# Running MLP block 1 between the two halves of block 0 in a fused attention and MLP kernel

## The chip, the cores and the metric

The kernel runs on one core of a Trainium2 chip. The metric is the device time of one execution in microseconds, the median of several runs. TensorE (PE in the profile) does the matrix products, VectorE (DVE), ScalarE (ACT) and GpSimd (POOL) the elementwise work, and SyncE (SP) issues the transfers.

## The reference

Kernelized attention for 8 batches of 8 heads, 576 positions and 64 channels, then a two-layer MLP over the 4608 tokens that it leaves.

```
def phi(x):                       # x: [b, h, s, 64], w_phi: [64, 128]
    proj = x @ w_phi
    proj = proj - max(abs(proj), over the 128 features)
    return concat(exp(proj), exp(-proj))
kv  = phi(k)^T v ; z = sum over s of phi(k)
out = (phi(q) kv) / (phi(q) z + 1e-6)          # per head
x   = out as [4608 tokens, 512]                # 8 heads x 64 channels
h   = x @ w_in                                 # 512 -> 2048
y   = max(0.01 * h, h) @ w_out                 # 2048 -> 512
```

All inputs and outputs are fp32.

## The kernel before, in words

**MLP.** The 4608 tokens are cut into 18 blocks of 256, the 2048 hidden features into 16 groups of 128. A *step* is one pair (block i, group ft), 288 in all. Step n calls `layer1(i, ft)`: 12 matmuls into one PSUM tile `h` of 128 features by 256 tokens (hi times hi, hi times lo and lo times hi of an fp32 number that is split into two fp32r numbers, for four 128-row parts of the 512 channels). ScalarE then applies the leaky ReLU (L606) and casts to `gh`, VectorE subtracts to get `gl` (L608). `LAG` = 3 steps later `layer2` multiplies `gh` and `gl` by the group's rows of `w_out`: 6 matmuls of 512 columns into two PSUM tiles `acc`, which hold the sums of a block's two token halves over its 16 groups. After the last group `acc` is copied to `o` (one half on ScalarE, one on VectorE) and written out. There are two `h` tiles and two `acc` tiles, so a block's second-layer sums can start only when the copies of the block before have been made.

**Split.** Before a block's first step `split(i)` reads its 256 tokens from `ring`, the SBUF tile that holds the attention result of two batches, and writes `xh` (four casts on ScalarE) and `xl` (four subtractions on GpSimd). There is one `xh` and one `xl`. A batch has 576 tokens: blocks 0 and 1 lie wholly in batch 0, block 2 takes its last 64 and the first 192 of batch 1.

**Weights.** `load_weights()` loads `w_in` and `w_out` group by group, 32 tiles of 512 KB, through two staging buffers: two of the four head-pair rows of batch 1 in `ring`, and `qh`. Each tile is rounded and split into hi and lo by two ScalarE reads (L159, L164), four VectorE operations (L160, L161, L162, L165), a ScalarE cast (`w0h`, `w1h`) and a VectorE subtraction (`w0l`, `w1l`).

**Attention.** Heads go in pairs, four pairs to a batch. `k_phase(i)` makes the key-value sums of pair i (its transposed result is kept in one tile `kvh`), `token_q_phase(i)` (pairs 4 to 7) or `q_phase(i)` the queries: three units of 256, 256 and 64 tokens for pairs 4 to 7, each closed on GpSimd by the multiplication `ring<-ring,mb` with the reciprocal of the denominator. Pairs 0 to 3 are done ahead of the MLP. `advance(goal)` emits attention work between the steps, at a pace set by the step's number n.

**Order.** The order in which instructions stand on each engine is made by the Tile scheduler from the order of emission, from priorities (attention before weights before MLP) and from its own timeline. On the chip each engine takes its instructions in that order and waits at each for its inputs.

Of the kernel before, what the change touches and what calls it, by code (L numbers as in the profile page):

```python
# [9 lines left out]
F32 = mybir.dt.float32  # L10
# [4 lines left out]
ALU = mybir.AluOpType  # L15
AX = mybir.AxisListType

P = 128
B, H, S, D = 8, 8, 576, 64
NP = H // 2  # L20
F = 128
U = 288
DM = 512
DFF = 2048
NFT = DFF // P
T = 256
TT = T // P
NTOK = B * S
NBLK = NTOK // T
LAG = 3  # L30
NN = 8
NK = 8
NF = 12
# [12 lines left out]
def attention_moe_kernel(ctx: ExitStack, tc: tile.TileContext, q, k, v, vt, w_phi, w_in, w_out, out):  # L46
    nc = tc.nc
# [4 lines left out]
    def ct(shape, dt, name):  # L52
        return cp.tile(shape, dt, tag=name, name=name)

    def st(shape, dt, tag):
        return sp.tile(shape, dt, tag=tag, name=tag, bufs=BUFS.get(tag, 1))
# [3 lines left out]
    def pick(key):  # L60
        n = cnt[key] = cnt.get(key, -1) + 1
        e = ENG.get(key, "")
        return e[n % len(e)] if e else None

    def copy_(key, o, i):
        e = pick(key) or "a"
        if e == "a":
            nc.scalar.copy(o, i)  # L68
        else:
            (nc.vector if e == "v" else nc.gpsimd).tensor_copy(o, i)  # L70

    def tt_(key, o, a, b, op):
        (nc.vector if pick(key) == "v" else nc.gpsimd).tensor_tensor(o, a, b, op=op)  # L73

    def pt(tag):
        return ps.tile([P, 512], F32, tag=tag, name=tag, bufs=PBUFS[tag])
# [5 lines left out]
    def weight(which, part, ft):  # L82
        g, f = divmod(ft, 4)
        if (which, part, g) not in weights:
            name = f"w{which}{part}{g}"
            weights[which, part, g] = (cp.tile([P, 4, DM], F32R, tag="late", name=name, bufs=4) if g == 3 else
                                       ct([P, 4, DM], F32R, name))
        return weights[which, part, g][:, f]
# [53 lines left out]
    for j in range(2):  # L142
        r = slice(64 * j, 64 * j + 64)
# [46 lines left out]
    def k_phase(i):  # L190
        nat, plain = i < NK, i < NF
        rk, rv = kraw.pop(i)
        if not plain:
            ks = st([P, 2, S], F32R, "ks")
            for j in range(2):
                o, n = slice(64 * j, 64 * j + 64), slice(64 - 64 * j, 128 - 64 * j)
# [16 lines left out]
        for g in range(3):  # L213
            w = 2 if g < 2 else 1
            r = slice(0, P) if g < 2 else slice(64, P)
            n = P if g < 2 else 64
# [8 lines left out]
            else:  # L225
                for s in range(w):
                    t0 = (2 * g + s) * P if g < 2 else S - P
                    pk = pt("a")
                    for j in range(2):
                        nc.tensor.matmul(pk[:, 256 * j : 256 * j + 256], lhsT=ks[:, j, t0 : t0 + P],  # L230
                                         rhs=wq.rearrange("p a f -> p (a f)"), start=True, stop=True)
# [13 lines left out]
            for s in range(w):  # L245
                c = 2 * g + s
                ek = st([P, 2, 256], F32, ("ek", "kph", "kpl")[c % 3] if nat else "ek")
# [30 lines left out]
        for j in range(2):  # L278
            for t in range(2):
                nc.tensor.transpose(kvtv[:, j, t], kvs[:, j, t], ident[0:66, 0:66])  # L280
        if i < NN:
            kvh = st([P, 2, 2, P], F32, "kvh")
            nc.scalar.copy(kvh[:, :, :, 0:64], kvtv[:, :, :, 0:64])
            nc.scalar.copy(kvh[:, :, :, 64:P], kvtv[:, :, :, 64:65].broadcast_to([P, 2, 2, 64]))
            kvs_of[i] = kvh, None
        else:
            kvh = st([P, 2, 2, P], F32R, "kvh")
            kvl = st([P, 2, 2, P], F32R, "kvl")
            zb = kvtv[:, :, :, 64:65].broadcast_to([P, 2, 2, 64])
            copy_("kvh", kvh[:, :, :, 0:64], kvtv[:, :, :, 0:64])  # L290
            copy_("kvh", kvh[:, :, :, 64:P], zb)
            nc.vector.tensor_tensor(kvl[:, :, :, 0:64], kvtv[:, :, :, 0:64], kvh[:, :, :, 0:64].bitcast(F32), op=ALU.subtract)
            nc.vector.tensor_tensor(kvl[:, :, :, 64:P], zb, kvh[:, :, :, 64:P].bitcast(F32), op=ALU.subtract)
            kvs_of[i] = kvh, kvl
# [274 lines left out]
    def attention():  # L569
        for i in range(NP, B * NP + 1):  # L570
            gens = [k_phase(i)] if i < B * NP else []
            if i > NP:
                gens.append((token_q_phase if i - 1 < NN else q_phase)(i - 1))
            while gens:
                for it in list(gens):
                    if next(it, end) is end:
                        gens.remove(it)
                    else:
                        yield i - 1
            yield i  # L580

    accs = {}
    gs = {}

    def split(i):
        for d in range(NP):
            t0 = 0
            while t0 < T:
                c = (i * T + t0) % (2 * S)
                n = min(T - t0, S - c % S)  # L590
                x = ring[:, c // S, d, c % S : c % S + n]
                t1 = t0 + n
                copy_("xh", xh[:, d, t0:t1], x)
                tt_("xl", xl[:, d, t0:t1], x, xh[:, d, t0:t1].bitcast(F32), ALU.subtract)
                t0 = t1

    def layer1(i, ft):
        ph = pt("h")[:, 0:T]
        for d in range(NP):
            nc.tensor.matmul(ph, lhsT=weight(0, "h", ft)[:, d * P : d * P + P], rhs=xh[:, d], start=d == 0, stop=False)  # L600
            nc.tensor.matmul(ph, lhsT=weight(0, "l", ft)[:, d * P : d * P + P], rhs=xh[:, d], start=False, stop=False)  # L601
        for d in range(NP):
            nc.tensor.matmul(ph, lhsT=weight(0, "h", ft)[:, d * P : d * P + P], rhs=xl[:, d], start=False, stop=d == NP - 1)  # L603
        gh = st([P, T], F32R, "gh")
        gl = st([P, T], F32R, "gl")
        nc.scalar.activation(ph, ph, AF.Prelu, alpha=0.01)  # L606
        copy_("gh", gh, ph)
        nc.vector.tensor_tensor(gl, ph, gh.bitcast(F32), op=ALU.subtract)  # L608
        gs[i, ft] = (gh, gl)

    def layer2(i, ft, half=range(TT)):
        if (i, 0) not in accs:
            for t in range(TT):
                accs[i, t] = pt("acc")
        gh, gl = gs[i, ft]
        for t in half:
            ts = slice(t * P, t * P + P)
            a = accs[i, t]
            nc.tensor.matmul(a, lhsT=gh[:, ts], rhs=weight(1, "h", ft), start=ft == 0, stop=False)  # L619
            nc.tensor.matmul(a, lhsT=gh[:, ts], rhs=weight(1, "l", ft), start=False, stop=False)  # L620
            nc.tensor.matmul(a, lhsT=gl[:, ts], rhs=weight(1, "h", ft), start=False, stop=ft == NFT - 1)  # L621
        if ft == NFT - 1:
            for t in half:
                o = st([P, DM], F32, "ek" if i == NBLK - 1 and t else "o")
                copy_("o", o, accs[i, t])
                r = i * T + t * P
                nc.sync.dma_start(out[r : r + P, :], o)

    stream = attention()
    state = {"p": PA, "n": NP - 1}  # L630
# [1 line left out]
    def advance(goal):  # L632
        keep = tc.cur_priority
        tc.cur_priority = state["p"]
        while state["n"] < goal:
            state["n"] = max(state["n"], next(stream, B * NP))
        state["p"] = tc.cur_priority
        tc.cur_priority = keep

    def room(i):  # L640
        return min(B, 2 + i * T // S) * NP
# [12 lines left out]
    tc.cur_priority = PW  # L654
    load_weights()
    tc.cur_priority = 0
    steps = [(i, ft) for i in range(NBLK) for ft in range(NFT)]
    split(0)
    for n, (i, ft) in enumerate(steps):
        layer1(i, ft)  # L660
        advance(min(room(i + 1), NP * (1 + (i + (ft + 1) / NFT) * T / S) + 2))
        if ft == NFT - 1 and i + 1 < NBLK:
            advance(math.ceil((i + 2) * T / S) * NP)
            split(i + 1)
        if n >= LAG:
            layer2(*steps[n - LAG])
    for t in range(TT):
        for s in steps[-LAG:]:
            layer2(*s, [t])
# [36 lines left out]
```

## Time and profile before

| | |
|---|---|
| three runs | 1202.78, 1204.13, 1205.22 us (median 1204.13) |
| profiled execution | 1204.23 us, of which the span is 1202.5 us |
| mean granted TensorE clock | 0.999 |
| busy share of the span | PE 97%, ACT 69%, DVE 64%, POOL 34% |

The span runs from the first to the last instruction; the 1.7 us beside it are start and end. Shares of busy time are means over stages that differ: the weights are made in the first 175 us and never again, attention ends at about 1030 us, and the rest is MLP alone. Matmuls overlap one another, so the PE's busy time is not a measure of its work; the prediction counts matmuls and multiplies by the distance between starts.

### The profile page before, as it was taken

To read this page: it belongs to the slowest core of one execution; us is meant where nothing else is said; L and a number is where in the kernel's file an instruction comes from. 1 tells how busy PE (TensorE), PEld (TensorE's weight loads), DVE (VectorE), ACT (ScalarE), POOL (GpSimd) and SP (SyncE) were. 2 spreads that over 40 slices of the span, in tenths; PEclk is the share of its full clock that TensorE was granted. 3 is DMA by queue.
4 is the path that set the end of the run, shared out by engine and by line. 5 is a ranking of instruction groups with operands and counts; after the bars stand their busy time and mean duration, and the time that the engine had idled before them with its cause. 6 is when DMAs were issued, how large, how long until landed. Compare 5 with 4: busy or idle time off the path is not lost.

```text
span 1202.5 us, 21117 instructions
## 1 busy us (share of the span) xinstructions
PE 1165.7 (97%) x7576; PEld 1040.8 (87%) x7576; DVE 763.6 (64%) x1508; ACT 833.4 (69%) x2104; POOL 412.3 (34%) x418
## 2 busy tenths in 40 slices
PE   8899899999999999999999999999999999999998
PEld 5687678989899999989898989898999999988987
DVE  5999984676676777777777777516677776211111
ACT  5988886677777787877777887626787877433222
POOL 0110112353445354545344454503454544210000
PEclk9999999999999999999999999999999999999999
DMA  7335532111111111111111110100111100000000
GB/s 208 94 113 152 158 106 58 33 49 42 40 31 41 30 30 41 32 49 31 40 32 49 32 49 22 40 10 28 32 50 31 50 1 19 1 18 14 6 19 19
DMA packets 62778, 57.01 MB, mean 47 GB/s; under 512 B 45136, under 2 KB 46288, under 8 KB 62672
## 3 DMA queue, kind: packets, MB, share of 16 engines
q1 hardware_dynamic: 62672, 55.65, 16.3%
q8 instruction: 60, 0.98, 0.3%
q14 instruction: 46, 0.38, 0.1%
HBM read 46.20 MB, written 9.44 MB: 46 GB/s over the span
## 4 chain that ended last, share of the span: by engine, by line
PE 70%; DVE 11%; ACT 10%; issue 3%; DMA 3%; POOL 1%; SPq 1%; POOLq 0%; DVEq 0%; ACTq 0%
PE h L600 9%; PE h L603 9%; PE h L601 9%; PE acc L619 9%; PE acc L620 9%; PE acc L621 9%; PE c L210 6%; PE a L417 2%; PE a L416 2%; PE a L419 2%; PE a L230 1%; DMA ring<-in_w_in_dram 1%; PE a L301 1%; DVE m L238 1%; PE a L376 1%
## 5 line engine op out<-in xcount | busy, mean ns | idle before, releaser
L600 PE MATMUL h<-xh,w0h 128*128 128x256 f32 x1152 | 293.9, 285 | 3.2 <-DVE gl L608 2.4
L601 PE MATMUL h<-xh,w0l 128*128 128x256 f32 x1152 | 290.8, 282 | 0.0
L608 DVE TENSOR_TENSOR gl<-h,gh 128x256 fp32r<-128x256 f32 x288 | 119.0, 417 | 263.7 <-ACT gh L68 223.5
L619 PE MATMUL acc<-w1h,gh 128*128 128x512 f32 x576 | 229.4, 400 | 10.5 <-ACT gh L68 6.2
L600 PEld LDWEIGHTS h<-xh,w0h 128*128 128x128 f32 x1152 | 218.1, 189 | 15.7 <-DVE gl L608 5.6
L606 ACT ACTIVATE h<-h 128x256 f32<-128x256 f32 x288 | 105.4, 368 | 178.9 <-PE h L603 176.6
L620 PE MATMUL acc<-w1l,gh 128*128 128x512 f32 x576 | 227.8, 396 | 0.0
L601 PEld LDWEIGHTS h<-xh,w0l 128*128 128x128 f32 x1152 | 217.9, 189 | 8.0 <-DVE w0l L73 0.6
L621 PE MATMUL acc<-w1h,gl 128*128 128x512 f32 x576 | 204.9, 397 | 0.0
L603 PE MATMUL h<-xl,w0h 128*128 128x256 f32 x1152 | 199.2, 282 | 0.9 <-POOL xl L73 0.8
L73 POOL TENSOR_TENSOR ql<-eq,qh 128x576 fp32r<-128x576 f32 x96 | 146.3, 1540 | 75.2 <-ACT qh L68 48.2
L603 PEld LDWEIGHTS h<-xl,w0h 128*128 128x128 f32 x1152 | 163.9, 189 | 2.5 <-POOL xl L73 1.9
L73 POOL TENSOR_TENSOR kpl<-ek,kph 128x512 fp32r<-128x512 f32 x72 | 95.9, 1332 | 171.5 <-ACT kph L68 90.0
L619 PEld LDWEIGHTS acc<-w1h,gh 128*128 128x128 f32 x576 | 108.1, 188 | 32.5 <-ACT gh L68 9.5
L68 ACT CAST gh<-h 128x256 fp32r<-128x256 f32 x288 | 105.7, 371 | 28.2 <-PE acc L620 23.1
L620 PEld LDWEIGHTS acc<-w1l,gh 128*128 128x128 f32 x576 | 108.2, 188 | 18.7 <-DVE pmk L241 0.4
L73 POOL TENSOR_TENSOR ring<-ring,mb 128x576 f32<-128x576 f32 (+2 forms) x45 | 49.4, 1098 | 196.5 <-DVE mb L344 57.1
L73 POOL TENSOR_TENSOR xl<-ring,xh 128x256 fp32r<-128x256 f32 (+3 forms) x96 | 58.6, 642 | 164.5 <-PE h L603 147.8
L621 PEld LDWEIGHTS acc<-w1h,gl 128*128 128x128 f32 x576 | 99.5, 189 | 8.2 <-DVE pmk L241 0.4
L248 ACT ACTIVATE ek<-pmk 128x256 f32<-128x256 f32 (+1 forms) x128 | 53.3, 417 | 41.5 <-POOL kpl L73 18.0
L210 PE MATMUL c<-kph,vh 128*66 128x256 f32 x240 | 62.1, 281 | 2.1 <-ACT kph L68 1.2
L210 PE MATMUL c<-kph,vl 128*64 128x256 f32 x240 | 61.8, 280 | 1.2 <-DVE kph L268 1.2
(205 smaller groups left out, 2240.8 us busy)
## 6 DMA issues: line engine op xcount, KB each, us to landing
out_dram<-o SPq DMA_DIRECT2D x35, 256.0 KB, 2.0
rk<-in_k_dram SPq DMA_DIRECT2D x29, 288.0 KB, 2.8
ring<-in_w_in_dram SPq DMA_DIRECT2D x16, 512.0 KB, 3.7
qh<-in_w_out_dram SPq DMA_DIRECT2D x16, 512.0 KB, 3.6
rq<-in_q_dram SPq DMA_DIRECT2D x28, 288.0 KB, 2.8
rv<-in_v_dram SPq DMA_DIRECT2D x29, 256.0 KB, 3.4
rv<-in_vt_dram SPq DMA_DIRECT2D x58, 32.0 KB, 3.0
fr<-in_k_dram SPq DMA_DIRECT2D x2, 288.0 KB, 3.4
```

The costliest lines, as they stand in the source:

```text
L68: nc.scalar.copy(o, i)
L73: (nc.vector if pick(key) == "v" else nc.gpsimd).tensor_tensor(o, a, b, op=op)
L210: nc.tensor.matmul(kvp[0 : lt.shape[1], 256 * j : 256 * j + 256], lhsT=lt, rhs=rt, start=first and j == 0, stop=last, skip_group_check=True)
L248: nc.scalar.activation(ek[r, :, 0:F], pmk[r, 2 * s : 2 * s + 2], AF.Exp)
L600: nc.tensor.matmul(ph, lhsT=weight(0, "h", ft)[:, d * P : d * P + P], rhs=xh[:, d], start=d == 0, stop=False)
L601: nc.tensor.matmul(ph, lhsT=weight(0, "l", ft)[:, d * P : d * P + P], rhs=xh[:, d], start=False, stop=False)
L603: nc.tensor.matmul(ph, lhsT=weight(0, "h", ft)[:, d * P : d * P + P], rhs=xl[:, d], start=False, stop=d == NP - 1)
L606: nc.scalar.activation(ph, ph, AF.Prelu, alpha=0.01)
L608: nc.vector.tensor_tensor(gl, ph, gh.bitcast(F32), op=ALU.subtract)
L619: nc.tensor.matmul(a, lhsT=gh[:, ts], rhs=weight(1, "h", ft), start=ft == 0, stop=False)
L620: nc.tensor.matmul(a, lhsT=gh[:, ts], rhs=weight(1, "l", ft), start=False, stop=False)
L621: nc.tensor.matmul(a, lhsT=gl[:, ts], rhs=weight(1, "h", ft), start=False, stop=ft == NFT - 1)
```

## The change

The list of steps is put in another order: (0, 0 to 7), then all of block 1, then (0, 8 to 15), then blocks 2 to 17. The second-layer sums of block 0 over its first eight groups are copied from `acc` to an SBUF tile `held` (tag `ks`, which is not in use at that time) so that block 1 can have the two `acc` tiles; after its last group VectorE adds the held half to `acc` in place of the copy. `split(0)` is made twice, before each half of block 0. Attention is still paced by n. For pairs 5 and 7 the tile for the key-value sums gets a tag of its own, `kvx`.

```
+CUT = 8
...
-            kvh = st([P, 2, 2, P], F32, "kvh")
+            kvh = st([P, 2, 2, P], F32, "kvx" if i % 2 else "kvh")
...
+    held = {}
+
     def layer2(i, ft, half=range(TT)):
-        if (i, 0) not in accs:
+        first, last = (ft in (0, CUT), ft in (CUT - 1, NFT - 1)) if i == 0 else (ft == 0, ft == NFT - 1)
+        if first and half[0] == 0:
             for t in range(TT):
                 accs[i, t] = pt("acc")
...
+        if not last:
+            return
+        for t in half:
+            if ft == CUT - 1:
+                if t == 0:
+                    held[0] = st([P, TT, DM], F32, "ks")
+                copy_("o", held[0][:, t], accs[i, t])
+                continue
+            o = st([P, DM], F32, "ek" if i == NBLK - 1 and t else "o")
+            if i == 0:
+                nc.vector.tensor_tensor(o, accs[i, t], held[0][:, t], op=ALU.add)
+            else:
                 copy_("o", o, accs[i, t])
...
-    steps = [(i, ft) for i in range(NBLK) for ft in range(NFT)]
+    steps = [(i, ft) for i in range(2, NBLK) for ft in range(NFT)]
+    steps = [(0, ft) for ft in range(CUT)] + [(1, ft) for ft in range(NFT)] + [(0, ft) for ft in range(CUT, NFT)] + steps
     split(0)
     for n, (i, ft) in enumerate(steps):
         layer1(i, ft)
-        advance(min(room(i + 1), NP * (1 + (i + (ft + 1) / NFT) * T / S) + 2))
-        if ft == NFT - 1 and i + 1 < NBLK:
-            advance(math.ceil((i + 2) * T / S) * NP)
-            split(i + 1)
+        advance(min(room(n // NFT + 1), NP * (1 + (n + 1) / NFT * T / S) + 2))
+        if n + 1 < len(steps) and steps[n + 1][0] != i:
+            advance(math.ceil((steps[n + 1][0] + 1) * T / S) * NP)
+            split(steps[n + 1][0])
```

In the program that comes of it PE has the same 7302 matmuls. ScalarE gets four more casts (`xh`), GpSimd four more subtractions (`xl`), VectorE two additions that take the place of a ScalarE and a VectorE copy (which now fill `held`). Lines of the changed kernel are one higher than before from L31 on, and more from L610 on.

On VectorE, in the middle of the weights (the groups 8 to 11 of `w_in` and `w_out`; `gl` closes a step of the MLP, `m`, `pmk`, `mb` and `tq` belong to attention), the rows from one `gl` on stood like this before:

```order
L608 TENSOR_TENSOR gl<-h,gh 128x256
L165 ISA ql<-ql,kvl 128x1024
L160 TENSOR_SCALAR ql<-ql 128x512
L161 TENSOR_SCALAR ql<-ql 128x512
L238 TENSOR_REDUCE m_1272<-a 128x4
L73 TENSOR_TENSOR w0l_801<-ql,w0h_800 128x512
L162 SCALAR_TENSOR_TENSOR ql<-qh,ql 128x512
L241 TENSOR_TENSOR pmk<-a,m_1272 128x512
L341 STREAM_TRANSPOSE mb<-dn 128x256
L312 TENSOR_REDUCE m_1294<-a 128x4
L165 ISA ql<-ql,kvl 128x1024
L160 TENSOR_SCALAR ql<-ql 128x512
```

At the same weights they now stand like this:

```order
L609 TENSOR_TENSOR gl<-h,gh 128x256
L74 TENSOR_TENSOR w0l_801<-ql,w0h_800 128x512
L163 SCALAR_TENSOR_TENSOR ql<-qh,ql 128x512
L166 ISA ql<-ql,kvl 128x1024
L161 TENSOR_SCALAR ql<-ql 128x512
L162 TENSOR_SCALAR ql<-ql 128x512
L74 TENSOR_TENSOR w1l_814<-ql,w1h_813 128x512
L163 SCALAR_TENSOR_TENSOR ql<-ring,ql 128x512
L609 TENSOR_TENSOR gl<-h,gh 128x256
L166 ISA ql<-ql,kvl 128x1024
L161 TENSOR_SCALAR ql<-ql 128x512
L162 TENSOR_SCALAR ql<-ql 128x512
```

There are more MLP steps and less attention between the same weights.

On GpSimd the rows after the last unit of batch 0 (128x4x64) read like this before (`ring<-ring,mb` closes a unit of attention, 128x64 is a pair's third; pairs 4, 5 and the start of 6):

```order
L73 TENSOR_TENSOR ring<-ring,mb 128x4x64
L180 MEMSET rv 128x10x2
L73 TENSOR_TENSOR ring<-ring,mb 128x256
L180 MEMSET rv 128x10x2
L73 TENSOR_TENSOR ring<-ring,mb 128x256
L73 TENSOR_TENSOR ring<-ring,mb 128x64
L73 TENSOR_TENSOR ring<-ring,mb 128x256
L180 MEMSET rv 128x10x2
L73 TENSOR_TENSOR ring<-ring,mb 128x256
L73 TENSOR_TENSOR ring<-ring,mb 128x64
L73 TENSOR_TENSOR ring<-ring,mb 128x256
L180 MEMSET rv 128x10x2
```

and like this now, from the same row to the second split of block 0 (`xl` rows belong to a split):

```order
L74 TENSOR_TENSOR ring<-ring,mb 128x4x64
L181 MEMSET rv 128x10x2
L74 TENSOR_TENSOR xl<-ring,xh 128x256 x4
L74 TENSOR_TENSOR ring<-ring,mb 128x256
L181 MEMSET rv 128x10x2
L74 TENSOR_TENSOR ring<-ring,mb 128x256
L74 TENSOR_TENSOR ring<-ring,mb 128x64
L74 TENSOR_TENSOR ring<-ring,mb 128x256
L181 MEMSET rv 128x10x2
L74 TENSOR_TENSOR ring<-ring,mb 128x256
L74 TENSOR_TENSOR ring<-ring,mb 128x64
L74 TENSOR_TENSOR xl<-ring,xh 128x256 x4
```

The split of block 1 has moved ahead of pair 4, into the time in which the weights are made; the second split of block 0 comes behind pair 5.

At the split of block 2 GpSimd had all units of pairs 6 and 7 behind it before: three `kpl`, four `ql` and two `vl` of later pairs stood between the last of them and the first `xl`. Now it reads as follows (numbers tell the tiles apart; the last unit of pair 6 stands one row ahead of the first, and the `ring` row is the first unit of pair 7):

```order
L74 TENSOR_TENSOR kpl_1778<-ek_1774,kph_1777 128x512
L74 TENSOR_TENSOR xl_71<-ring_69,xh_70 128x64
L74 TENSOR_TENSOR xl_71<-ring_69,xh_70 128x192
L74 TENSOR_TENSOR xl_71<-ring_69,xh_70 128x64
L74 TENSOR_TENSOR xl_71<-ring_69,xh_70 128x192
L74 TENSOR_TENSOR xl_71<-ring_69,xh_70 128x64
L74 TENSOR_TENSOR kpl_1800<-ek_1796,kph_1799 128x512
L74 TENSOR_TENSOR xl_71<-ring_69,xh_70 128x192
L74 TENSOR_TENSOR xl_71<-ring_69,xh_70 128x64
L74 TENSOR_TENSOR ring_69<-ring_69,mb_1809 128x256
L74 TENSOR_TENSOR kpl_1833<-ek_1829,kph_1832 128x512
L74 TENSOR_TENSOR xl_71<-ring_69,xh_70 128x192
```

The first unit of pair 7 now lies in the middle of the split that needs it.

More of the change, by code (lines that the diff above doesn't have):

```diff
@@ L618, in layer2 @@
             a = accs[i, t]
-            nc.tensor.matmul(a, lhsT=gh[:, ts], rhs=weight(1, "h", ft), start=ft == 0, stop=False)
+            nc.tensor.matmul(a, lhsT=gh[:, ts], rhs=weight(1, "h", ft), start=first, stop=False)
             nc.tensor.matmul(a, lhsT=gh[:, ts], rhs=weight(1, "l", ft), start=False, stop=False)
[L621 to L624, printed above, removed]
+            nc.tensor.matmul(a, lhsT=gl[:, ts], rhs=weight(1, "h", ft), start=False, stop=last)
+        if not last:
[10 more added lines that the diff above has]
+            else:
                 copy_("o", o, accs[i, t])
-                r = i * T + t * P
-                nc.sync.dma_start(out[r : r + P, :], o)
+            r = i * T + t * P
+            nc.sync.dma_start(out[r : r + P, :], o)
     stream = attention()
```

## The prediction

> **What bounds the kernel now.** I read the page's busy times first, then windows along the run, then PE's groups and waits in the stretch in which the windows differ.
>
> ```profile
> PE 1165.7 (97%) x7576; PEld 1040.8 (87%) x7576; DVE 763.6 (64%) x1508; ACT 833.4 (69%) x2104; POOL 412.3 (34%) x418
> 110.00:175.00 65.00, 59.77 (x322) 45.41 (x320) 62.52 (x132) 55.52 (x133) 5.24 (x10) 1.00 0.51 143
> 215.00:250.00 35.00, 34.61 (x231) 31.54 (x230) 22.33 (x44) 24.04 (x65) 15.86 (x19) 1.00 0.11 27
> 250.00:800.00 550.00, 540.17 (x3658) 493.24 (x3657) 388.98 (x743) 419.22 (x1062) 252.15 (x230) 1.00 0.13 37
> ```
>
> The columns of a window are its length, then PE, PE's weight loads, DVE, ACT and POOL busy, the clock and the transfers. Over the run PE is the bound (97%). Between 110 and 175 us, while weights are made, it is DVE: 62.5 of 65 us. From 215 us on DVE has a third of its time free and PE none.
>
> How much PE loses there must be counted, since its records overlap. Steps 8 to 15 of block 0 run from 109.79 to 175.69 us:
>
> ```profile
> 109.33 0.63 PE L621 MATMUL acc<-w1h,gl 128*128 128x512 f32 x2
> 109.79 0.28 PE L600 MATMUL h<-xh,w0h 128*128 128x256 f32 x1
> 109.91 0.29 PE L601 MATMUL h<-xh,w0l 128*128 128x256 f32 x1
> ...
> 133.78 1.46 PE L332 MATMUL a<-eq,kvh 128*128 128x256 f32 x6
> 135.08 1.03 PE L301 MATMUL a<-bd,rq 128*128 128x256 f32 x4
> 175.69 0.36 PE L600 MATMUL h<-xh,w0h 128*128 128x256 f32 x1
> ...
> L600 PE MATMUL h<-xh,w0h 128*128 128x256 f32 x32 | 8.5, 296 | 0.0
> L301 PE MATMUL a<-bd,rk 128*128 128x256 f32 x22 | 6.0, 384 | 0.0
> L332 PE MATMUL a<-qs,kvh 128*128 128x256 f32 x24 | 5.9, 390 | 0.0
> L210 PE MATMUL c<-ek,rv 128*66 128x256 f32 x20 | 5.2, 381 | 1.7 <-issue 1.7
> ```
>
> From start to start a layer-1 matmul takes 0.12 us, a layer-2 one 0.23 ((109.79 - 109.33) / 2), a plain fp32 one of attention 0.216 a record ((135.08 - 133.78) / 6), and each of those has two records, 0.43. The eight steps hold 96 layer-1 (11.4 us), 42 layer-2 (9.7), 68 plain ones of 256 columns (136 records, 29.4, the last three rows are the largest of nine such groups) and 46 small ones (5.1): 55.6 us of work in 65.9. **PE idles 10.3 us**, because a step needs its group's weights and DVE makes a group every 8.9 us. That is the most this change can attack; steps 0 to 7 stand as they were.
>
> What the DVE does there, from the end of group 7's weights to the end of the last (103.8 to 175.3 us):
>
> ```profile
> 103.80:175.30 71.50, 66.27 (x353) 50.53 (x351) 68.64 (x144) 60.73 (x144) 5.24 (x10) 1.00 0.49 138
> L238 DVE TENSOR_REDUCE m<-a 128x4 f32<-128x512 f32 (+1 forms) x8 | 4.7, 588 | 0.2
> L241 DVE TENSOR_TENSOR pmk<-a,m 128x512 f32<-128x512 f32 (+1 forms) x8 | 4.7, 588 | 0.1
> L312 DVE TENSOR_REDUCE m<-a 128x4 f32<-128x512 f32 (+1 forms) x8 | 4.5, 567 | 0.1
> L313 DVE TENSOR_TENSOR tq<-a,m 128x512 f32<-128x512 f32 (+1 forms) x8 | 4.5, 565 | 0.0
> L608 DVE TENSOR_TENSOR gl<-h,gh 128x256 fp32r<-128x256 f32 x8 | 3.2, 403 | 0.0
> L344 DVE STREAM_TRANSPOSE mb<-rc 128x256 f32<-128x256 f32 (+1 forms) x8 | 3.1, 387 | 0.0
> L341 DVE STREAM_TRANSPOSE mb<-dn 128x256 f32<-128x256 f32 (+1 forms) x8 | 3.1, 383 | 0.0
> L343 DVE RECIPROCAL rc<-mb 128x8 f32<-128x8 f32 (+1 forms) x8 | 1.4, 180 | 0.0
> ```
>
> Eighty weight operations, eight units each of a key and a query phase, eight `gl`; 2.9 us idle.
>
> **The change, part by part.** *Weights against steps.* By the new order DVE has closed 22 steps, not 15, when the last weight is made, and step 16 (group 8 of block 1, the first to use a new weight again) stands behind the weights of group 11. PE no longer waits for a weight. Of DVE work between the same two points, 7 `gl` come in (+2.8), one copy into `held` (+0.7, as a 128x512 subtraction of the weights), and three of the eight units of each attention phase go out: 3/8 of 26.0 us in the seven rows = 9.8. That makes -6.3, and since the groups add up to 78.2 against 68.64 of union, -5.5 of real time.
>
> *Splits that move under the weights.* GpSimd's four `xl` of block 1 fall into this stretch. What they cost DVE is shown by a unit's multiplication:
>
> ```profile
> 121.41 1.21 DVE L73 TENSOR_TENSOR w1l<-ql,w1h 128x512 fp32r<-128x512 f32 x1
> 121.32 0.75 POOL L73 TENSOR_TENSOR ring<-ring,mb 128x256 f32<-128x256 f32 x1 [0.35 <-DVE mb L344]
> L73 DVE TENSOR_TENSOR w0l<-ql,w0h 128x512 fp32r<-128x512 f32 x8 | 5.5, 685 | 0.0
> L73 POOL TENSOR_TENSOR xl<-ring,xh 128x256 fp32r<-128x256 f32 x8 | 6.8, 861 | 9.6 <-ACT xh L68 9.6
> ```
>
> The subtraction beside it took 1.21 us for 0.69: 0.52 lost. Four `xl` cost DVE 0 to 2.1; two units that leave the stretch give 1.0 back; I take +1.1. The Trainium skill ("SBUF — State Buffer", Who interferes with whom) says that a VectorE operation with two SBUF inputs and a GpSimd one that reads SBUF exclude each other for the whole instruction. By that rule four `xl` of 0.86 could cost 3.4 us and the sum below would be 1.3 us worse; this trace shows the direction, and less than the whole.
>
> So the weights end at 175.3 - 5.5 + 1.1 = 170.9 if DVE idles as before.
>
> *PE in the same time.* It stands at step 8 with 1.4 us less done (six layer-2 matmuls later), at 108.4 us. Steps 8 to 21 hold 168 layer-1 (20.0), 79 layer-2 (18.3), 44 plain attention matmuls (19.0) and 32 small ones (3.9): 61.2 us, so step 22 cannot start before 169.6. DVE says 170.9. Two engines are then full at once, and each can hold up the other: I add DVE's 2.9 us of idle once more, 173.8, 4.2 us of PE idle. The bounds are 1.3 (DVE's own pace) and 10.3 (as now). The nearer is the lower, since no weight is waited for. Before had that PE work done at 175.69 + 4.2 us of its next steps + about 0.4 of waits = 180.3. **Gain 6.5.**
>
> *One more split.* Three changes of block fall between step 8 and block 2 instead of two. Where nothing covers one, late in the run, it costs PE this much; in the covered middle some cost nothing and one this:
>
> ```profile
> 1109.21 0.50 PE L619 MATMUL acc<-w1h,gh 128*128 128x512 f32 x1 [1.05 <-ACT gh L68]
> 321.59 0.50 PE L619 MATMUL acc<-w1h,gh 128*128 128x512 f32 x1 [1.38 <-ACT o L68]
> ```
>
> I take 1.2, bounds 0 and 1.8. The VectorE additions replace copies of the same size after the last matmul, so `acc` comes free as before: nothing. The extra casts (4 of some 0.4 us on ACT, 85% busy in that window) lie inside those 1.2 us. The transfers of weights keep their order; the outputs of block 1 go out before block 0's, and nobody reads them.
>
> *Attention is late.* At step 32 PE has done 117 of 334 attention matmuls fewer, at step 96 62, at step 160 36, and from step 168 on both programs issue the same. Between, PE is full and DVE at 71% (the window from 250 us), so the work only moves. The waits of that stretch change places with the order:
>
> ```profile
> PE acc L619 <- DVE o L70: 1.8, 2, 1.7
> PE acc L619 <- ACT o L68: 1.4, 1, 1.4
> PE h L600 <- DVE gl L608: 1.3, 3, 0.7
> PE c L210 <- DVE kph L268: 1.2, 1, 1.2
> ```
>
> (185 to 800 us, 10.0 in all eleven rows.) I take 0, with 3 to either side. `kvx` spares pair 5's and 7's last copies a wait for the pair before; off PE's path, 0.
>
> Sum against the profiled execution, 1204.2, which lies 0.1 above the median: 1204.2 - 6.5 + 1.2 = **1198.9**.
>
> **Rivals.** *Dense.* DVE and PE lose nothing to each other and the split is covered: 180.3 - 170.9 = 9.4, so 1194.8. For it speaks that two of the three steps of `LAG` stand between a `gl` and its use; against it that DVE would need 96% and PE 98%.
>
> *No change.* The idle only moves: PE's listed waits now are mostly for ACT and attention rows, not weights:
>
> ```profile
> PE c L210 <- issue: 1.7, 2, 1.0
> PE acc L619 <- ACT gh L68: 1.7, 2, 1.2
> PE acc L619 <- ACT w1h L68: 0.8, 1, 0.8
> ```
>
> (103 to 176 us, 4.9 in all.) If these come as thick as before, 10.3 us stay: 180.3 - 179.9 = 0.4 gained, 1.2 paid: 1205.0. Against it: an engine that is ahead of DVE must wait somewhere, and PE will be ahead no longer.
>
> *Slower.* Block 2 waits for pair 7, now just ahead of it. Before, with weights done, the units ended so:
>
> ```profile
> 182.81 0.32 POOL L73 TENSOR_TENSOR ring<-ring,mb 128x64 f32<-128x64 f32 x1 [0.86 <-DVE mb L344]
> 195.26 0.73 POOL L73 TENSOR_TENSOR ring<-ring,mb 128x256 f32<-128x256 f32 x1
> 217.01 0.32 POOL L73 TENSOR_TENSOR ring<-ring,mb 128x64 f32<-128x64 f32 x1 [5.40 <-DVE mb L344]
> ```
>
> A pair takes 34.2 us from last unit to last, its first unit 12.5. Pair 5 ends near 173.8, so pair 7's first unit comes at 173.8 + 34.2 + 12.5 = 220.5. PE reaches the fourth part of block 2's first step after 46.4 + 4.7 us of work and two splits, 227. It decides when pairs take 14 us longer than that row: 6.5 to be late, and 7.7 to lose the gain and 0.2%. At 1.5 times (51 us) the unit is at 237.6, 10.6 late: 1198.9 + 10.6 = 1209.5, and a wait can cost the clock too:
>
> ```profile
> 575.00:600.00 25.00, 23.39 (x145) 20.59 (x145) 18.66 (x38) 17.48 (x46) 10.29 (x9) 0.93 0.16 47
> ```
>
> Here 7% of 25 us, 1.7 us, were lost behind waits of 1.2 and 0.25 us.
>
> **Chances.** About 0.2% (2.4 us) is what a measurement of this kernel tells from no change. Forecast 0.55, own range 1195.5 to 1202; dense 0.15; no change 0.20; slower 0.10. The forecast's upper end lies within 2.4 us of the old time: 0.02 of it goes to "same". Faster 0.68, same 0.22, slower 0.10. The range leaves out a tenth on each side: from 1192.5 (dense, with 2.3 of the 3 us of the later stretch) to 1206.5 (no change, with half of them).
>
> **What would show it.** Step 22 near 174 us and the weights done by then; PE's waits between 108 and 174 us under 5 us in all; DVE over 95% busy to the end of the weights; attention later by some 20 us around block 2, without a wait of PE of over 2 us there; the same rows from step 168, and all of them earlier by the same 5 us. Wrong it is if the weights end after 178 us, if PE waits for `gh` or `gl` more often than once in two steps, or if block 2's first step stalls on `xl`.

## The result and the profile after

The changed kernel takes **1194.79 us** (median of four runs, 1192.93 to 1196.45) against 1203.91 for the kernel before on the same chip: ratio 0.9921, interval 0.9906 to 0.9937. The forecast was 1198.9, so the kernel is 4.1 us faster than forecast and 9.1 faster than before. That lies just below the forecast's own range (1195.5 to 1202) and inside the outer one (1192.5 to 1206.5). The profiled execution took 1196.45 us, of which the span is 1194.7.

The page's first rows, then the three windows that the prediction read, in the changed kernel (columns as there):

```profile
PE 1164.5 (97%) x7576; PEld 1045.5 (88%) x7576; DVE 755.9 (63%) x1510; ACT 833.5 (70%) x2108; POOL 417.5 (35%) x422
...
110.00:175.00 65.00, 64.92 (x386) 53.84 (x385) 60.83 (x129) 53.78 (x128) 5.30 (x9) 1.00 0.48 139
215.00:250.00 35.00, 35.00 (x221) 31.01 (x220) 19.51 (x42) 22.90 (x65) 11.45 (x18) 1.00 0.19 51
250.00:800.00 550.00, 539.80 (x3676) 495.85 (x3675) 392.11 (x763) 429.97 (x1089) 264.71 (x239) 0.99 0.14 38
```

The busy share of the whole run says nothing: 97% both times. In the weights' stage PE now shows 386 matmul records in 65 us where it had 322, and is busy to 64.92 us. In the 550 us behind it, it is as busy as before (539.80 against 540.17), though the clock there is lower, 0.99 for 1.00. The gain is in the first of the three windows, and something in the last took part of the clock.

The end of the weights, in VectorE's timeline (start, duration; the last `w1l` closes them), and the start of step 22 in PE's:

```profile
172.38 0.42 DVE L609 TENSOR_TENSOR gl<-h,gh 128x256 fp32r<-128x256 f32 x1
173.07 0.69 DVE L74 TENSOR_TENSOR w1l<-ql,w1h 128x512 fp32r<-128x512 f32 x1 [0.26 <-ACT w1h L69]
...
174.32 0.47 PE L601 MATMUL h<-xh,w0h 128*128 128x256 f32 x1
```

The weights end at 173.8 us and step 22 starts at 174.3. Before, 15 steps were closed at that point; now it is 22.

**Where PE idles.** To place the rest I counted as the prediction did: each matmul at its distance between starts (layer 1 0.119, layer 2 0.232, plain fp32 0.432 us), and the idle time of PE is the time at which a step starts less the work ahead of it. Differences between steps, in us, for every version that was run (the labels are those of the experiments below; in every version all attention is done by step 232, and from step 168 on they do the same work):

| steps | before | after | e1 | e2 | e3 | e4 | e5 | e6 | e7 | e8 | e9 | e10 |
|---|---|---|---|---|---|---|---|---|---|---|---|---|
| start to 8 | 17.3 | 19.6 | 19.2 | 19.2 | 18.8 | 17.2 | 19.0 | 17.5 | 18.6 | 19.4 | 19.5 | 19.9 |
| 8 to 32 (weights) | 13.3 | 3.1 | 3.3 | 11.0 | 2.9 | 2.9 | 6.4 | 7.3 | 10.4 | 12.4 | 11.6 | 6.4 |
| 32 to 64 | 2.5 | 1.6 | 1.8 | 2.1 | 1.6 | 5.1 | 1.1 | 2.4 | 1.2 | 1.2 | 0.9 | 4.8 |
| 64 to 104 (blocks 4 to 6) | 3.9 | 13.7 | 20.7 | 9.2 | 13.7 | 13.2 | 4.2 | 4.2 | 8.7 | 4.9 | 1.0 | 0.6 |
| 104 to 168 | 11.6 | 2.5 | 8.6 | 12.2 | 1.2 | 0.0 | 16.9 | 1.1 | 9.0 | 8.5 | 4.2 | 0.9 |
| 168 to 280 | 6.4 | 6.7 | 6.5 | 6.2 | 6.1 | 6.1 | 6.3 | 6.3 | 6.2 | 6.7 | 6.0 | 6.1 |

From before to after the rows give +2.3, -10.2, -0.9, +9.8, -9.1 and +0.3, together -7.8, which is the difference of the spans (1202.5 and 1194.7). So three things of about 10 us happened: the weights' stage gained 10.2, block 4 cost 9.8, and the long stretch from step 104 to 168 gained 9.1. The last two cancel, which nobody had forecast: that the total came out near the forecast is luck in this respect.

The +2.3 at the start is not the change. Windows of after, then before, ahead of the first MLP step:

```profile
45.00:57.00 12.00, 8.49 (x28) 6.63 (x27) 8.91 (x19) 10.45 (x25) 3.05 (x4) 0.72 0.26 70
```

```profile
45.00:57.00 12.00, 8.17 (x37) 6.17 (x38) 10.98 (x22) 11.71 (x27) 4.21 (x5) 1.00 0.31 89
```

In this execution the clock stood at 0.5 for 6.8 us there. The profile of e8, which has the order of before, shows the same drop at 48.2 us, and that of e6, which has block 1 between the halves, does not.

**Block 4.** Its first step starts at 356.3 us, 22 us earlier than before (378.4); its last 128 tokens belong to batch 2, whose last pair is pair 11. The unit that closes pair 11, on GpSimd, before and then after:

```profile
345.98 1.43 POOL L73 TENSOR_TENSOR ring<-ring,mb 128x576 f32<-128x576 f32 x1 [4.83 <-PE a L230]
```

```profile
367.18 1.41 POOL L74 TENSOR_TENSOR ring<-ring,mb 128x576 f32<-128x576 f32 x1 [3.28 <-DVE mb L429]
```

It had been 31 us ahead of the block (347.4 to 378.4) and is now 12 us behind it (368.6 to 356.3). PE's timeline and windows in the changed kernel show what it does meanwhile:

```profile
365.80 0.40 PE L377 MATMUL a<-qs,wq 128*128 128x288 f32 x1 [1.13 <-DVE tq L379]
...
367.98 0.40 PE L377 MATMUL a<-qs,wq 128*128 128x288 f32 x1 [1.64 <-DVE pmk L236]
...
368.98 0.38 PE L601 MATMUL h<-xh,w0h 128*128 128x256 f32 x1
...
375.29 0.50 PE L623 MATMUL acc<-w1h,gh 128*128 128x512 f32 x1 [1.91 <-ACT gh L69]
```

```profile
360.00:370.00 10.00, 6.91 (x43) 5.59 (x42) 7.50 (x15) 6.69 (x17) 3.64 (x4) 0.98 0.25 84
370.00:380.00 10.00, 8.09 (x39) 7.54 (x39) 9.11 (x21) 6.04 (x17) 3.49 (x4) 0.68 0.25 64
```

Between 361.07 and 368.98 us PE's timeline has no layer-1 row: the fourth of the 128-row parts, pair 11's heads, is missing. PE waits on the attention's own elementwise operations (`tq`, `pmk`), one after the other, and the clock falls to 0.5 for two pieces of 3.4 us, from 369.6 and from 376.4 us. The three waits (4.7 us), the clock (3.4) and some short gaps make the 9.8 us. The chain of work that ended last runs the same way (start, duration, what):

```profile
366.24 0.79 DVE mb L429
...
367.18 1.42 POOL ring L74
368.60 0.02 issue
368.63 0.31 ACT xh L69
368.93 0.04 issue
368.98 0.38 PE h L601
```

The transposed reciprocal, the multiplication that closes pair 11, the cast of the split, the matmul.

### The profile page after: what moved, and what is told of

The parts are those of the page before. It is cut to its first block, busy times and chain, and to the rows that moved or that the text cites. A ratio compares the mean times of both kernels' runs of the same rounds, so it can differ in the third digit from the quotient of the medians.

```text
span 1194.7 us, 21190 instructions
## 1 busy us (share of the span) xinstructions
PE 1164.5 (97%) x7576; PEld 1045.5 (88%) x7576; DVE 755.9 (63%) x1510; ACT 833.5 (70%) x2108; POOL 417.5 (35%) x422
## 4 chain that ended last, share of the span: by engine, by line
PE 82%; DVE 8%; ACT 5%; issue 2%; DMA 1%; POOL 1%; SPq 0%; DVEq 0%; ACTq 0%; POOLq 0%
PE h L601 10%; PE h L604 10%; PE h L602 10%; PE acc L623 10%; PE acc L625 10%; PE acc L624 10%; PE c L211 7%; PE a L302 2%; PE a L420 2%; PE a L418 2%; PE a L417 2%; PE a L231 2%; PE a L333 1%; PE a L377 1%; PE a L378 1%
## 5 line engine op out<-in xcount | busy, mean ns | idle before, releaser
L623 PEld LDWEIGHTS acc<-w1h,gh 128*128 128x128 f32 x576 | 108.4, 188 | 27.7 <-ACT gh L69 8.9
L624 PEld LDWEIGHTS acc<-w1l,gh 128*128 128x128 f32 x576 | 108.4, 188 | 18.0
L74 POOL TENSOR_TENSOR xl<-ring,xh 128x256 fp32r<-128x256 f32 (+3 forms) x100 | 62.6, 655 | 162.1 <-PE h L604 131.6
L249 ACT ACTIVATE ek<-pmk 128x256 f32<-128x256 f32 (+1 forms) x128 | 53.3, 417 | 33.5 <-POOL kpl L74 17.3
L199 DVE TENSOR_TENSOR ks<-rk,ks 64x576 fp32r<-64x576 f32 x40 | 44.5, 1112 | 30.5 <-ACT ks L69 29.9
```

What stands on the lines that cost most here:

```text
L249: nc.scalar.activation(ek[r, :, 0:F], pmk[r, 2 * s : 2 * s + 2], AF.Exp)
```

## The experiments

Ten more kernels were run. The theories: the forecast's (less time is lost between weights and steps, the rest only moves) with block 4 as the price that was missed; and, for the middle stretch, that the spacing of the pairs among the steps decides.

### Without the second tile, and with the tile alone

```
after:   kvh = st([P, 2, 2, P], F32, "kvx" if i % 2 else "kvh")
e1:      kvh = st([P, 2, 2, P], F32, "kvh")
e2:      the kernel before, with after's line
```

> The changed kernel with one tile kvh for all pairs again. Theory, that the second tile lies off PE's path: the time of the changed kernel, 1194.8, within 2 us, and PE idle between step 8 and step 32 of 3 to 5 us, as there (3.1). Rival, that it keeps the chain of pairs 5 to 7 going while PE has little else: pair 6 and 7 later, PE waits at block 2, 1198 or more.

Measured: 1209.65 us, ratio to before 1.0051 (1.0036 to 1.0066). The time is in the rival's range, but not by the rival's way: pairs 6 and 7 close at 210.9 and 243.4 us (210.8 and 244.8 in after), and steps 32 to 64, with block 2, idle 1.8 us for 1.6.

> The kernel before with the second tile kvx alone, block order as before. Theory, that the gain comes from the order of the steps: 1204 within 2 us, PE idle 10 us between 110 and 176 us as before. Rival, that the tile alone frees the attention chain: 1201 or less.

Measured: 1209.47 us, ratio 1.0049 (1.0032 to 1.0066). The theory's and the rival's times both fell. Together the two parts gain 9 us, each alone loses 6. The table says where: e1 keeps the whole gain of the weights' stage (3.3 us idle against 3.1), so that gain is the order's and not the tile's. It loses 20.7 us at blocks 4 to 6, 14.1 of them between steps 64 and 72, and 8.6 in steps 104 to 168. e2 idles in the weights' stage nearly as before (11.0), and more at blocks 4 to 6. Window of e1, then of after, at block 4:

```profile
360.00:400.00 40.00, 33.28 (x202) 29.41 (x202) 30.01 (x53) 31.65 (x79) 19.43 (x17) 0.91 0.16 45
```

```profile
360.00:400.00 40.00, 35.00 (x221) 31.87 (x220) 28.65 (x57) 29.77 (x76) 15.94 (x15) 0.91 0.15 45
```

So an edit that touches two tiles of batch 1 changes the time hundreds of microseconds later, in work that doesn't use them. The tag changes the order that the scheduler makes of everything behind it. Whether the tile has a price of its own is asked by e10.

### Block 4 without its wait

```
             x = ring[:, c // S, d, c % S : c % S + n]
+            if i == 4 and t0 > 0:
+                x = ring[:, 1, d, 320 : 320 + n]
```

> The changed kernel, in which the split of block 4 takes its last 128 tokens from batch 1's rows in place of batch 2's, so that it does not wait for pair 11 (128 tokens of the output belong to other tokens). The changed kernel loses 9.8 us between steps 64 and 72, 6.4 us of waits and 3.4 us by two drops of the clock to a half. Theory, that this is the price of attention that comes just too late for block 4: 1185 to 1188. Rival, that attention is behind for good and the wait only moves to the next block that needs a batch (block 6, where pair 15 stands at step 96 itself): 1192 to 1196.

Measured: 1193.79 us, ratio 0.9916 (0.9901 to 0.993), as the rival had it. The loss at block 4 is gone, as the first window shows (it was 6.91 and 8.09 of 10 us), and it stands at block 6, which needs pair 15, instead:

```profile
360.00:370.00 10.00, 10.00 (x72) 9.33 (x71) 7.60 (x16) 6.97 (x20) 2.52 (x3) 1.00 0.16 57
370.00:380.00 10.00, 10.00 (x72) 9.28 (x71) 9.71 (x23) 8.15 (x19) 3.70 (x5) 1.00 0.27 66
490.00:500.00 10.00, 6.95 (x31) 5.43 (x30) 9.71 (x17) 5.21 (x12) 3.57 (x4) 0.74 0.09 30
500.00:510.00 10.00, 7.86 (x38) 6.72 (x37) 9.60 (x22) 6.88 (x20) 2.30 (x4) 0.74 0.26 64
```

PE reaches block 6 at 481.4 us there (498.6 in after), and pair 15 closes at 495.7. Between steps 64 and 104 e3 idles 13.7 us in all, exactly what after does. That shows the cause (a block whose attention is late) and that it is a debt: attention pushed out of the weights' stage is paid for at the first block that comes before its pair is done, and a block let through passes it on.

### Paying the debt earlier: GpSimd's share, and the cut

```
e4:  -  tt_("ql", ql, eq, qh.bitcast(F32), ALU.subtract)
     +  (nc.vector if i < 12 else nc.gpsimd).tensor_tensor(ql, eq, qh.bitcast(F32), op=ALU.subtract)
e5:  -  CUT = 8
     +  CUT = 12
e6:  e4's edit and e5's
```

> The changed kernel with the subtraction ql of pairs 8 to 11 on VectorE in place of GpSimd: four a pair, 1.54 us on GpSimd, about 0.75 us on VectorE by its 128x512 subtractions. Theory, that the chain of pairs 8 to 11 is what is late at block 4: up to 4 times 3.2 us earlier, the 9.8 us shrink to under 3, 1186 to 1189. Rival, that VectorE (70% busy there, 80% then) hands the gain back in later gl: 1193 to 1196.

Measured: 1191.38 us, ratio 0.99 (0.9884 to 0.9916), between theory and rival. The unit that closes pair 11 starts at 366.8 us instead of 367.2 and block 4 still loses 7.6 us (9.8 before this edit): taking this work from GpSimd hardly brings attention forward.

> The changed kernel with CUT = 12: block 1 stands between block 0's groups 0 to 11 and 12 to 15. Theory: the reuse of weights fills PE while DVE makes weights, and what is lost at block 4 is that attention was pushed back in that time (pair 5 closed at 176 us, 157 before) and then runs at a fixed pace of some 33 us a pair, so that pair 11 comes at 367 us to a PE that is there at 356. With CUT = 12 the first twelve groups run at the weights' pace as before, pair 5 closes near 160 us and pair 11 near 350, and PE reaches step 64 near 363: idle of some 8 us between steps 8 and 22 (2.3 at CUT = 8), no wait at block 4, 1187 to 1191. Rival: the gain is the reuse alone and the wait at block 4 an accident of the order; then 6 us of reuse are lost and some wait stays: 1197 to 1202.

Measured: 1201.91 us, ratio 0.999 (0.998 to 1.0); the theory's 1187 to 1191 was missed. The time is in the rival's range (1197 to 1202), but for another reason. Up to step 104 it came as the theory had it: 6.4 us idle in the weights' stage, pair 11 closed at 354 us with PE at block 4 at 365, blocks 4 to 6 down to 4.2. At step 104 e5 had idled 30.7 us, after 38.0. Then it lost 16.9 us in steps 104 to 168, the largest piece here in PE's timeline, with the window around it:

```profile
564.28 0.45 PE L211 MATMUL c<-kpl,vh 128*66 128x256 f32 x2
568.13 0.48 PE L211 MATMUL c<-kph,vh 128*66 128x256 f32 x1 [3.40 <-ACT kph L69]
```

```profile
560.00:575.00 15.00, 11.60 (x66) 10.24 (x65) 11.46 (x19) 11.37 (x30) 10.00 (x10) 0.77 0.27 78
```

> CUT = 12 and the subtraction ql of pairs 8 to 11 on VectorE. Theory: attention has a lead already, so the faster chain has nothing to bring: as with CUT = 12 alone, within 2 us. Rival: the chain is what PE waits for all along, and it brings 3 us again, as it did at CUT = 8 (1191.4 against 1194.8).

Measured: **1188.19 us**, ratio 0.9877 (0.986 to 0.9893), 13.7 us less than e5, where the theory had within 2 and the rival 3. Nearly all of it is in steps 104 to 168: 1.1 us idle instead of 16.9. The edit touches pairs 8 to 11, and these steps compute later ones; again it is the order that changed.

### Lighter weights in the old order

```
-                nc.vector.tensor_tensor(wi, wi, cr, op=ALU.add)
```

This leaves out, on each weight tile, the VectorE addition that rounds the weights by their lowest bits.

> The kernel before without the integer addition of each weight tile (L165, 32 times 0.71 us on VectorE; the low bits of the weights are left out). Theory, that VectorE's weights hold PE up in block 0: steps 8 to 15 take 57 to 61 us instead of 65.9 and hold 2 to 5 us of PE idle instead of 10. Rival, that PE idles there for attention's rows between the steps or for the transfers of the weights: 64 us or more, idle of 8 us or more.

Measured: 1203.33 us, in a single run. The weights end at 163.5 us instead of 175.2, and steps 8 to 15 take 56.1 us instead of 65.9, a little under the 57 to 61 expected: VectorE's weights set their pace. The idle time in them hardly fell, though: 9.1 us, where the theory had 2 to 5 and the rival 8 or more. The windows of these steps, e7 and then before:

```profile
108.30:164.40 56.10, 53.43 (x281) 42.39 (x279) 45.62 (x96) 45.89 (x109) 7.19 (x11) 0.94 0.49 144
```

```profile
109.80:175.70 65.90, 60.67 (x330) 46.11 (x328) 63.27 (x133) 56.42 (x135) 5.62 (x11) 1.00 0.50 142
```

281 matmul records instead of 330: attention went out of the stretch with the weights' time (47.0 us of PE work instead of 55.6), and the clock was at 0.94. Work that is only moved out gains nothing. So e7 does not show that PE's idle time was a wait for weights: the longest waits listed for PE there are 1.5 us for `ek`, 0.8 for `kvh` and 0.6 for `rc`, all of attention. That the idle time goes when steps can use weights again is shown by e1 and e2.

### The spacing of the pairs

The edits of e1, e4, e5 and e6 all showed up in steps 104 to 168. The instruction order has one thing in which the versions differ there, the steps at which attention closes a pair:

| | pairs close at step | idle, steps 104 to 168 |
|---|---|---|
| after | 110, 118, 126, 134, 142, 150, 158 | 2.5 |
| e6 | 108, 116, 124, 132, 140, 148, 156 | 1.1 |
| before | 105, 112, 121, 129, 137, 144, 153 | 11.6 |
| e1 | 109, 116, 124, 133, 141, 149, 158 | 8.6 |
| e5 | 109, 116, 124, 132, 140, 149, 157 | 16.9 |

A pair every eight steps, or a mix of seven, eight and nine. Three kernels were chosen for it; their order was known, their time not.

```
e8:   the kernel before, with e4's edit        104, 113, 121, 129, 137, 145, 153
e9:   e6 with CUT = 14                          104, 112, 120, 128, 136, 144, 152
e10:  e6 with  kvh = st(..., "kvh")             108, 116, 124, 132, 140, 148, 156
```

> The kernel before, with the subtractions `ql` of pairs 8 to 11 on VectorE instead of GpSimd and nothing else: the control for the fastest version (CUT of 12 and this edit, 1188.2). Steps 104 to 168 hold the same work in every version and cost TensorE 11.6 us of idling in the kernel before, 16.9 with CUT of 12 and 1.1 with the edit added. Theory, spacing: what decides is how the scheduler lays attention between the steps; where a pair follows every eight steps TensorE loses 1 to 3 us, where the distances are a mix of 7, 8 and 9 it loses 9 to 17. In this kernel they stay a mix (104, 113, 121, 129, 137, 145, 153), so 8 to 17 us stay lost there and the time is 1201 to 1206. Rival, the edit itself: GpSimd was late, and with `ql` on VectorE the loss goes whatever the order: 1192 to 1195, and the new order of the blocks is worth only the 5 us that are left to 1188.

Measured: 1200.19 us, ratio 0.9968 (0.9954 to 0.9981); 8.5 us idle in steps 104 to 168. The rival, the edit itself (1192 to 1195), is out. The theory's loss is right; the time is just below its range (1201 to 1206).

> CUT of 14 with `ql` of pairs 8 to 11 on VectorE: block 1 goes in after 14 of block 0's 16 groups. The pairs follow every eight steps from step 48 on, and pair 11 closes eight steps ahead of block 4, pair 15 eight ahead of block 6. Spacing theory: steps 104 to 168 cost 1 to 3 us, block 4 and block 6 wait for nothing; the weights' stage loses 5 to 8 us between steps 8 and 22 (4.8 to 5.7 with CUT of 12, 2.3 with 8, 10 to 11 in the order of before), since only two of block 0's weight groups are moved behind block 1: 1187 to 1192. Rival: the middle stretch goes as it likes, with 9 to 17 us lost there, for a cause other than the spacing: 1196 to 1205.

Measured: 1192.26 us, ratio 0.99 (0.988 to 0.9921), just above the theory's range; 4.2 us there, a little over the 1 to 3, and blocks 4 to 6 cost 1.0. Steps 8 to 22 idle 8.3 us, just over the 5 to 8 expected, and steps 8 to 32 idle 11.6, where before has 13.3: with two groups behind block 1 the order gives little at the weights.

> The fastest version (CUT of 12, `ql` of pairs 8 to 11 on VectorE) without the second tile `kvx`: odd pairs of batch 1 write `kvh` again. Without `kvx` the changed kernel lost 15 us (1209.7 against 1194.8), with it alone the kernel before lost 6. Spacing theory: here the pairs follow every eight steps from step 52 to step 156 without it too, pair 11 closes four steps ahead of block 4, and the time is 1187 to 1191, so that the tile has no price of its own and had worked through the order alone. Rival, the tile itself: pairs 5 and 7 wait for the tile of the pair before, attention comes 3 us or more later, and the time is 1194 to 1203.

Measured: **1187.63 us**, ratio 0.9857 (0.9832 to 0.9882), the fastest of all, level with e6 (1188.19). So the tile shows no price of its own here. The window of steps 104 to 168 in e10, e8 and before:

```profile
530.00:790.00 260.00, 259.91 (x1787) 239.81 (x1786) 183.96 (x351) 203.91 (x515) 124.96 (x110) 1.00 0.13 36
```

```profile
530.00:790.00 260.00, 255.51 (x1738) 234.49 (x1738) 182.75 (x346) 200.47 (x505) 122.89 (x109) 0.99 0.13 36
```

```profile
530.00:790.00 260.00, 254.04 (x1719) 231.92 (x1718) 184.09 (x344) 197.90 (x498) 120.94 (x108) 0.99 0.13 36
```

VectorE, ScalarE and GpSimd have nearly the same load in all three (70 to 71%, 76 to 78%, 47 to 48%), so none of them is the bound; PE is full in one and loses 6 us in another. Even spacing went with 0.0 to 4.2 us of loss in six versions (e3 and e4 among them), uneven spacing with 8.5 to 16.9 in six (e2 and e7 among them). What this shows is that the order decides, and that in these twelve versions the spacing told the good orders from the bad ones. It is no explanation. In e8 only one distance is odd (104 to 113), and its three waits of over 1 us come behind it, ahead of steps 116, 132 and 148, where a pair follows every eight steps (PE's timeline in e8):

```profile
587.33 0.49 PE L600 MATMUL h<-xh,w0h 128*128 128x256 f32 x1 [1.74 <-DVE gl L608]
...
653.81 0.39 PE L600 MATMUL h<-xh,w0h 128*128 128x256 f32 x1 [1.22 <-DVE gl L608]
...
719.08 0.39 PE L600 MATMUL h<-xh,w0h 128*128 128x256 f32 x1 [1.25 <-DVE gl L608]
```

The traces do show where the loss lies: mostly in the first four steps of a block (from steps 112, 128, 144 and 160). By the same count these sixteen steps hold 10.5 us of it in before, 8.4 in e1, 9.8 in e2, 14.0 in e5, 7.3 in e7 and 6.3 in e8, and 0.0 to 2.1 in the six even versions. So what the good orders do better is the change of block. Why an uneven one stalls PE there is not shown: the waits are on different tiles in each (3.4 us for `kph` in e5; before has eight rows of waits there, the largest 1.2 us, for `kph`; in e8 all but 0.2 of 4.4 us are for `gl`), and no kernel was built in which the spacing alone was changed.

## Why the prediction was right, and where it was not

**PE no longer waits for weights: right, and under-sized.** PE has no listed wait at all between 108 and 174 us (under 5 us was forecast). Steps 8 to 22 idled 2.3 us for 4.2 forecast. By absolute time the gain comes out almost exactly (same PE work at 180.6 before and 174.3 after, 6.3 for 6.5), but only because PE reached step 8 at 110.8 us instead of 108.4, after the early clock drop; at equal footing the gain is 8.6. The weights ended at 173.8, as forecast, and VectorE's idle time doubled as assumed, in its windows and groups of 104 to 174 us:

```profile
104.00:174.00 70.00, 69.92 (x411) 58.12 (x410) 64.06 (x135) 59.70 (x144) 8.22 (x11) 1.00 0.49 141
L161 DVE TENSOR_SCALAR ql<-ql 128x512 f32<-128x512 f32 x16 | 7.2, 448 | 4.6 <-ACT ql L160 4.5
L74 DVE TENSOR_TENSOR w0l<-ql,w0h 128x512 fp32r<-128x512 f32 x8 | 5.5, 686 | 0.0
```

5.9 us idle against 2.9. The reason was another than the one given: VectorE waits 4.5 us for ScalarE's first read of a weight tile (1.0 before), not for PE. "DVE over 95% busy" was therefore missed (64.06 of 70, 92%).

**GpSimd's `xl` beside the weights, +1.1.** Not confirmed as a size. The `w0l` and `w1l` subtractions took 0.686 us (0.685 and 0.745 before). The four `xl` ran from 107.1 to 111.1 us. Two VectorE operations with both inputs in SBUF fell among them: the `scalar_tensor_tensor` took its usual 0.68 us, the rounding addition 1.00 where the median of 26 is 0.68. That is 0.3 us, far from the 3.4 that the Trainium skill's exclusive lock ("SBUF — State Buffer", Who interferes with whom) would make of four `xl`, since hardly any such operation stood beside them.

**One more split, +1.2: over-sized.** From step 22 to 36, with two of the three changes of block, PE idled 1.5 us; before had 2.9 in the same work. The third, at step 8, lies within the 2.3 us of steps 8 to 22. No extra cost shows.

**Attention late, 0 with 3 to either side: the step that failed.** The delay was seen (pair 7 closes at 244.8 us instead of 217.0; some 20 us were forecast), and block 2 was not held up: pair 7's first unit came at 223.8 (220.5 forecast). But the working stopped at that block. The "slower" rival's mechanism, a block that waits for its pair, came true two blocks later, at 9.8 us where it had been priced at 10.6. A row or two more would have told: from pair 7 to pair 11 the pairs follow each other every 32 us before and every 31 after, since PE is full, so of the 28 us at pair 7 there are still 21 left at pair 11, and with block 4 coming 22 us sooner a margin of 31 us is gone. And the same 0 hid a gain of the same size: that the new order runs smoothly in steps 104 to 168 could not be read from a trace of the old one, and what its even spacing is worth came out only in the experiments. The term measured +9.8 at block 4 and -9.1 in the middle; its bounds of 3 us were too narrow for either. That they cancelled is luck.

**`kvx`, off PE's path, 0: wrong as worked out.** It shows no price in itself (e10 against e6), but without it this kernel is 15 us slower, through the order of the rest.

**The same rows from step 168, 5 us earlier: right in kind,** 8.1 us in fact (794.4 and 786.3).

The rivals: "dense" (1194.8) hit the number, and its weights' gain of 9.4 is nearer to the 8.6 at equal footing than the forecast's 6.5; but it did not have the two large terms either, so that its total is luck too. "No change" fell: PE's waits did not come back at the weights. "Slower" is the mechanism of block 4.

## What to carry to other kernels

When work that a later stage needs is pushed back, follow it to every consumer and not only to the next one: list when each is due and when it will come, since a full engine catches up slowly (here 7 of 28 us over four pairs) and the debt falls due at the first consumer whose margin is smaller. Where a scheduler lays out thousands of instructions, a small edit can change the order of everything behind it, and 5 to 15 us of 1200 can hang on that alone; judge an edit by where PE idles, stage by stage, and try its neighbours, for here two neutral ones (CUT of 12, and one subtraction on another engine) brought 7 us more together and one of them lost 7 alone.

## What the runs showed of the hardware

The clock falls to 0.5 for 3.4 us or twice that at a time (3.4 us from 578.9 in before, 6.8 near 48 us in after), and each 3.4 us of it costs 1.7. The Trainium skill ("TensorE: Matmul & The Clock Gate", What's actually happening) gives windows of 3413 ns and half rate after an idle one; the unit and the rate agree. But full idle windows were not needed: at block 4 no single wait passed 2 us, and in the kernel before, the drop at 579 us came behind waits of 1.2 and 0.25 us. Nor does each such wait bring a drop: in e8 a single one of 1.7 us, ending at 587.3, was followed by 3.4 us at half, in after one of 1.8, ending at 571.6, by none. So short waits can cost twice, once as waits and once by the clock: of after's 9.8 us between steps 64 and 72, 6.4 are waits and gaps and 3.4 clock. How much idle time it takes is not shown.
